# Convolution and SoLU block on one core: the prologue's order recast, w_out's low words on GpSimd, g in the mean's matrix, narrow products for the first eight tiles, the third tile in its own banks

## Chip, core and metric

The kernel runs on one core of a Trainium2 chip, in one launch. The engines named below are TensorE (PE, with its weight loads PEld), VectorE (DVE), ScalarE (ACT), GpSimd (POOL) and the queue of SyncE (SP), which issues the DMAs. The metric is the device time of one execution in microseconds; three executions were timed before the change.

## What is computed

Inputs are x (8 x 4160 x 192, float32), weight (8 heads x 7 taps), w_in (192 x 1024), w_out (1024 x 192) and g_ln (1024); the last three are float64, read by the kernel as pairs of 32-bit words.

```python
# 1. causal convolution over 7 rows, softmax weights per head (24 columns each)
w = softmax(weight, axis=-1)
out = einsum('hk,bskhg->bshg', w, x_unf)
# 2. h = x @ w_in, SoLU, layer norm, second product
h = x @ w_in
solu = h * softmax(h)
ln = (solu - mean(solu)) / sqrt(var(solu) + 1e-6) * g_ln
return (ln @ w_out).astype(float32)
```

## The kernel before

The 33,280 rows are 260 tiles of 128 rows. Each tile passes through these steps, every one a helper with a name: the first product `ph` (PE; `emit_rows` L736 and `emit_third` L759, eight and two or more matmuls of 512 columns), the maximum (`emit_max` L788, DVE), the exponential (`emit_exp` L795, ACT), the numerators h*e (`emit_mul` L805, DVE), their upper half in float16 (`emit_hi` L813, ACT), the lower half (`emit_lo` L825, POOL), a DMA transpose of both, the second product `po` (`emit_out` L841, PE), its evacuation (`emit_evac` L848, DVE), and a scaling per row and a store. All instructions are written out by hand in one order per engine (the schedule is manual), and each engine works through its own list strictly in order; semaphores carry the dependences, those of a buffer that is overwritten too.

The convolution works on chunks of up to 19 windows of 112 rows. Its product `pc` is made on PE (L281), its upper half is stored by ACT (`upper`, L313) and its lower half by DVE (`lower`, L322), and DMA transposes (`turn`, L352) bring both into `yT`, from which the tiles take their rows.

PSUM holds three pairs of banks (`pair(0)` to `pair(2)`), used in turn by the first products and by the convolution's early groups (`hold`), and two single banks for `po` and small sums.

Before the first tile stands a prologue. It makes the tap matrix; it turns the float64 words of w_in into float32 (`wi`: `exponents`, `mantissas`, `join`, `signs`, `value` on DVE; `powers`, `squares` on ACT), finds a power-of-two scale `t_in` from the sum of squares, and writes w_in in two float16 parts, `whi` and `wlo`. The same is done for w_out (`wo`), in part between the first tiles: `exponents` L447 and `mantissas` L452 on DVE, `lows` L458, `powers` L486 and `floats` L463 on ACT, `signs` L489 on DVE, `whole` L474 and `value` L496 on POOL. `signs` writes its result in place over the exponents `e_out`. Then `out_powers` (L685, ACT, eight instructions) multiplies `e_out` by g_ln, `squares` (L469, ACT) sums its squares for the scale `t_out`, a product with the constant matrix `even` gives the mean over rows of w_out (L701, PE), `out_upper` subtracts it (L710, DVE) and writes the upper half `ohi` (L715, ACT), `out_lower` (L719, DVE) the lower half `olo`.

The first eight tiles go two at a time (`first_two`, `second_two`, `third_two`, `fourth_two`), all later ones three at a time (`three_steps`). In `first_two` the tiles 0 and 1 use pairs 0 and 1, and pair 2 takes two groups of chunk 1's convolution; in `second_two` the tiles 2 and 3 use pairs 0 and 1 again. A `po` of a tile in a group of several tiles is 16 matmuls, eight of 384 columns (upper and lower half of w_out side by side) and eight of 192; the five last tiles have groups of one and use 24 matmuls of 192.

Of the kernel before, what the change touches and what calls it, by code (L numbers as in the profile page):

```python
# [19 lines left out]
def kernel(  # L20
# [102 lines left out]
    class Chunk:  # L123
# [185 lines left out]
        def upper(self, pc, h, n, a, b):  # L309

            col, cuts = h * HD, self.cut(h * HD, n * HD)
            for e, z in zip(cuts, cuts[1:]):
                act.activation(  # L313
                    self.at(0, col + e, col + z, a, b), pc[:, :, e:z], AF.Copy,
                    scale=self.scale(),
                )

# [77 lines left out]
    )  # L395

# [22 lines left out]
    even = cp.tile([P, P], F32, name="even")  # L419
    pool.memset(even, 1.0 / F)  # L420
# [6 lines left out]
    class Words:  # L427
# [29 lines left out]
        def lows(self, c, scale):  # L457
            act.activation(  # L458
                self.low[:, c].bitcast(F32), self.low[:, c], AF.Copy, scale=scale
# [5 lines left out]
        def squares(self, c, to):  # L465
# [4 lines left out]
                junk, self.e[:, c].bitcast(F32), AF.Square, scale=2.0**20, accum_out=to  # L470
# [65 lines left out]
    wi.powers(halves[0])  # L536

# [28 lines left out]
    words(halves[1])  # L566
    for h in c0.halves(1):
        c0.sum_squares(*h)
        if h[2] == 0:
            wi.powers(halves[1])  # L570
# [15 lines left out]
    isq = cp.tile([P, 2], F32, name="isq")  # L586
# [8 lines left out]
    def settle(a, z, got):  # L595
        for pc, hg in got:
            c0.lower(pc, *hg)
        for blk in (0, 2, 1):
# [8 lines left out]
    wi.signs(halves[0], wi.m)  # L607
    wi.exponents(Z)
    wi.powers(Z)
    for f in chain0[1:-3]:  # L610
        f()
    wi.squares(Z, isq[:, 1:2])
    for pc, hg in got0:
        c0.upper(pc, *hg)
    wi.value(halves[0], wi.m, dve)
    valued(halves[1])
    c0.open(0, None)
# [50 lines left out]
    def settle_rest():  # L668
        settle(*spans0[1], got0)
# [26 lines left out]
    def out_mean():  # L696
# [827 lines left out]
```

## Time and profile before

| | |
|---|---|
| median of three runs | 1181.34 us (1178.92 to 1181.7) |
| the profiled execution | 1182.51 us, of which the span from first to last instruction is 1180.7 us |
| busy over the span | PE 96%, DVE 87%, ACT 84%, POOL 74% |
| granted TensorE clock | 0.999 of full on average |

The busy shares are averages over two different kernels in one: the long stage of three tiles at a time, and the first 120 us, in which the prologue's work and the first tiles share the engines. The views of the second kind are the windows (busy time of each engine by stretch) and the timelines of single engines.

### The profile page before, as it was taken

How to read it: one execution, taken by the hardware profiler on the slowest of the kernel's cores; microseconds unless marked ns; L12 is line 12 of the kernel's file. 1: busy time of each engine (PE TensorE's matmuls, PEld its weight loads, DVE VectorE, ACT ScalarE, POOL GpSimd, SP SyncE). 2: the span in 40 equal slices, each digit the busy share in tenths (PEclk: the TensorE clock that was granted, in tenths of full speed). 3: DMA queues.
4: the chain of work that ended last, by engine and by line, in shares of the span. 5: the costliest groups of instructions: out<-in, count | busy, mean ns of one | idle time of the engine just before them, and what ended most of it. 6: DMA issues, size and time to landing. Idle time of an engine off the chain costs nothing.

```text
span 1180.7 us, 22219 instructions
## 1 busy us (share of the span) xinstructions
PE 1136.1 (96%) x7678; PEld 688.2 (58%) x7678; DVE 1027.5 (87%) x2072; ACT 997.1 (84%) x1758; POOL 876.7 (74%) x683
## 2 busy tenths in 40 slices
PE   5888999999999999999999999999999999999997
PEld 3455555565566555556556665655566556566555
DVE  7888888898899889898898989888898998788787
ACT  6997888888888888788888888888888888888885
POOL 1644878887978778797867878688788868855664
PEclk9999999999999999999999999999999999999999
DMA  7898899999999999999999999999999998999987
GB/s 196 187 183 157 154 220 200 207 185 204 192 212 205 184 197 186 209 197 197 208 187 214 187 211 200 189 204 192 220 190 194 195 202 167 180 171 193 180 159 174
DMA packets 727294, 226.94 MB, mean 192 GB/s; under 512 B 651518, under 2 KB 725774, under 8 KB 727182
## 3 DMA queue, kind: packets, MB, share of 16 engines
q1 hardware_dynamic: 727182, 225.53, 99.5%
q8 instruction: 60, 0.98, 0.3%
q14 instruction: 52, 0.43, 0.1%
HBM read 33.00 MB, written 25.56 MB: 50 GB/s over the span
## 4 chain that ended last, share of the span: by engine, by line
PE 70%; DVE 7%; DMA 6%; POOL 6%; issue 4%; ACT 4%; SPq 2%; ACTq 0%; POOLq 0%; DVEq 0%
PE po L841 32%; PE ph L736 29%; DMA pT<-p 5%; PE pc L281 4%; PE ph L759 4%; POOL p L825 4%; DVE ph L788 2%; DVE e L805 1%; ACT p L813 1%; DMA raw_in<-in_moe_w_in_dram 1%; SPq L827 1%; POOL t L909 1%; ACT e L795 1%; ACT sq L817 1%; DVE y L322 1%
## 5 line engine op out<-in xcount | busy, mean ns | idle before, releaser
L825 POOL TENSOR_TENSOR p<-e,p 128x1024 f16<-128x1024 f32 x259 | 552.4, 2137 | 243.8 <-ACT p L813 242.7
L841 PE MATMUL po<-ohl,pT 128*128 128x384 f16 (+1 forms) x4200 | 542.3, 285 | 16.3 <-DMA pT<-p 10.8
L841 PEld LDWEIGHTS <-pT 128*128 128x128 f16 x4200 | 380.2, 98 | 181.8 <-DMA pT<-p 13.9
L736 PE MATMUL ph<-whi,yT 128*128 128x512 f16 x1548 | 419.1, 380 | 6.0 <-DVE e L805 4.6
L788 DVE TENSOR_SCALAR_CACHE_REDUCE ph<-ph,cv 128x1024 f32<-128x1024 f32 x248 | 319.2, 1288 | 78.3 <-PE ph L759 61.7
L795 ACT ACTIVATE e<-ph,sm 128x1024 f32<-128x1024 f32 x260 | 289.2, 1112 | 105.2 <-DVE ph L788 98.6
L805 DVE SCALAR_TENSOR_TENSOR e<-ph,cv,e 128x1024 f32<-128x1024 f32 x248 | 317.0, 1278 | 22.6 <-ACT e L795 22.3
L736 PEld LDWEIGHTS <-yT 128*128 128x128 f16 x2064 | 192.4, 98 | 235.0 <-issue 34.9
L813 ACT CAST p<-e 128x1024 f16<-128x1024 f32 x260 | 269.9, 1039 | 39.0 <-DVE e L805 38.8
L817 ACT ACTIVATE sq<-e 128x1024 f32<-128x1024 f32 x260 | 273.5, 1052 | 0.1
L848 DVE TENSOR_REDUCE raw<-po 128x192 f32<-128x384 f32 x255 | 140.6, 552 | 15.9 <-PE po L841 15.6
L736 PE MATMUL ph<-wlo,yT 128*128 128x512 f16 x516 | 153.5, 379 | 0.0
L243 POOL TENSOR_TENSOR xs<-xr,xs 128x960 f16<-128x960 f32 (+1 forms) x56 | 107.5, 1920 | 1.4
L313 ACT ACTIVATE y<-pc 112x432 f16<-112x432 f32 (+5 forms) x140 | 62.7, 469 | 17.4 <-PE pc L281 11.7
L759 PE MATMUL ph<-wlo,yT 64*128 64x512 f16 x269 | 74.1, 380 | 1.1 <-DMA yT<-y 1.1
L281 PE MATMUL pc<-xs,taps_hi 128*112 128x240 f16 (+1 forms) x448 | 72.9, 261 | 1.4 <-DVE xm L203 1.4
L322 DVE SCALAR_TENSOR_TENSOR y<-pc,y 112x432 f16<-112x432 f32 (+5 forms) x140 | 72.2, 532 | 0.7 <-ACT y L313 0.7
L759 PE MATMUL ph<-wlo,y 64*128 64x512 f16 x251 | 68.5, 380 | 1.3 <-DMA y<-yT 1.3
L181 DVE TENSOR_REDUCE xa<-xr 128x1 f32<-128x384 f32 x112 | 66.6, 617 | 3.2 <-DMA xr<-in_x_dram 3.2
L281 PEld LDWEIGHTS <-taps_hi 128*112 128x112 f16 x448 | 52.4, 130 | 18.1 <-issue 1.7
L240 POOL TENSOR_SCALAR xr<-xr,s 128x960 f32<-128x960 f32 (+1 forms) x56 | 57.5, 1026 | 3.0
L281 PE MATMUL pc<-xs,taps_lo 128*112 128x240 f16 (+1 forms) x224 | 58.5, 261 | 0.0
(145 smaller groups left out, 783.9 us busy)
## 6 DMA issues: line engine op xcount, KB each, us to landing
out_dram<-raw SPq DMA_DIRECT2D x127, 192.0 KB, 3.0
xr<-in_x_dram SPq DMA_DIRECT2D x41, 480.0 KB, 5.1
xr<-in_x_dram SPq DMA_DIRECT2D x22, 384.0 KB, 4.1
pT<-p SPq DMA_TRANSPOSE x260, 4.7
y<-yT SPq DMA_DIRECT2D x15, 140.0 KB, 3.0
y<-yT SPq DMA_DIRECT2D x15, 126.0 KB, 3.0
yT<-y SPq DMA_TRANSPOSE x102, 3.7
raw_out<-in_moe_w_out_dram SPq DMA_DIRECT2D x1, 1536.0 KB
```

Of the source, the lines that this page charges most:

```text
L243: (2.1 * size + 0.2, lambda: pool.tensor_tensor(xl, r, h, ALU.subtract)),
L281: nc.tensor.matmul(o, tp[:, h + j, :], r, start=q == 0, stop=q == len(ops) - 1)
L736: nc.tensor.matmul(bank, lhs, w[:, r, n * 512 : (n + 1) * 512], start=start and j == 0, stop=stop and j == len(ops) - 1,)
L759: nc.tensor.matmul(banks_of(t)[n], y[q, t.off : t.off + P], wlo[q, 1, n * 512 : (n + 1) * 512], start=start, stop=not start,)
L788: dve.tensor_scalar(t.ph, t.ph, t.cv[:, 0:1], None, ALU.mult, ALU.min, accum_out=t.bias)
L795: act.activation(t.e, t.ph, AF.Exp, bias=t.bias, scale=-1.0, accum_out=grp.z[:, g : g + 1])
L805: dve.scalar_tensor_tensor(t.e, t.ph, t.cv[:, 3:4], t.e, ALU.mult, ALU.mult, accum_out=t.grp.s1[:, t.g : t.g + 1],)
L813: act.copy(t.p16[:, :, 0, :], t.halves)
L817: act.activation(junk, t.e, AF.Square, accum_out=t.grp.s2[:, t.g : t.g + 1])
L825: eng.tensor_tensor(t.p16[:, :, 1, :], t.halves, t.p16[:, :, 0, :], ALU.subtract)
L841: nc.tensor.matmul(t.po[:, 0:n], t.pT[:, a, :], w, start=j == 0, stop=j == len(ops) - 1)
L848: dve.tensor_reduce(t.grp.raw[:, t.g, :], t.po[:, 0 : 2 * D].rearrange("p (a d) -> p d a", a=2), AX.X, ALU.add,)
```

## The change

- `gl` (g_ln) is loaded right behind w_out instead of after chunk 1. `even` is no longer a constant: it is made on POOL from `gl` (a matrix per block of 128 rows, g/1024), in one of the four `p16` buffers.
- `wo.lows` moves from ACT to POOL, behind the small constants of tile 0.
- In the prologue w_in's first half is finished earlier (`valued(halves[0])`), its squares are taken in three parts, the convolution's first two groups stand together on PE ahead of the sum `pt_x`, the second part's groups ahead of the sum `pt_wi`, and the transposes of block 0 are issued as soon as the upper halves they need are written.
- `out_powers` is gone. `out_squares` takes its place: the largest |g| (two small DVE instructions) is the scale of `wo.squares`, which now stands ahead of `signs` and is written before it. `out_upper` becomes eight instructions of 192 columns with g as scalar instead of two of 768.
- `hold` of chunk 1's first two groups moves from `first_two` to `second_two`, into pair 1; tile 2 uses pair 2, tile 3 pair 0, and the later tiles keep that rotation.
- In `first_two` tile 0's `emit_hi` stands right behind its `emit_mul`, ahead of tile 1's exponential.
- The first eight tiles' `po` is 24 matmuls of 192 columns, and their evacuation a copy instead of a sum of two halves.

```diff
@@ prologue
-    even = cp.tile([P, P], F32, name="even")
-    pool.memset(even, 1.0 / F)
+    even = sp.tile([P, NH, 2, 512], F16, name="even", tag="p16", bufs=4)
...
+    pool.tensor_scalar(
+        even, gl.unsqueeze(2).broadcast_to([P, NFC, P]), 1.0 / F, 1.0,
+        ALU.mult, ALU.mult,
+    )
...
     words(halves[0])
     wi.powers(halves[0])
+    valued(halves[0])
...
-    going = convolve(*spans0[0], [pq[:, 0:512], pq[:, 512:F]])
-    got0 = [next(going)]
+    got0 = list(convolve(*spans0[0], [pq[:, 0:512], pq[:, 512:F]]))
     c0.add_up()
-    got0 += going
-    wi.squares(A, isq[:, 0:1])
...
+    wi.squares(halves[1], isq[:, 1:2])
+    c0.open(0, None)
+    ups = [f for pc, hg in got0 for f in c0.upper_steps(pc, *hg)]
+    for f in ups[:2]:
+        f()
+    c0.turn(0, *spans0[0])
     wi.exponents(Z)
     wi.powers(Z)
+    valued(halves[1])
+    wi.mantissas(Z)
+    wi.squares(Z, isq[:, 2:3])
...
-    wo.lows(W, 2.0**-32)
-    wi.mantissas(Z)
     wi.join(Z)
...
+    wo.lows(W, 2.0**-32)
     wo.mantissas(W)
@@ out_powers, out_upper
-    def out_powers():
-        woe = wo.e.bitcast(F32).rearrange("p (c d) -> p c d", d=D)
-        for j in range(NFC):
-            act.activation(
-                woe[:, j], woe[:, j], AF.Copy, scale=gl[:, j : j + 1]
-            )
+    def out_squares():
+        g = cp.tile([P, 1], F32, name="g_max")
+        dve.tensor_reduce(g, gl, AX.X, ALU.max, apply_absolute_value=True)
+        dve.tensor_scalar(g, g, 2.0**20, None, ALU.mult)
+        wo.squares(W, osq, g)
...
-            dve.scalar_tensor_tensor(
-                wof[:, c], wof[:, c], 1.0,
-                mean[:, 0:D].unsqueeze(1).broadcast_to([P, NFC // 2, D]),
-                ALU.mult, ALU.subtract,
-            )
+            for j in range(c.start, c.stop):
+                dve.scalar_tensor_tensor(
+                    wof[:, j], wof[:, j], gl[:, j : j + 1], mean[:, 0:D],
+                    ALU.mult, ALU.subtract,
+                )
@@ emit_out, emit_evac
+        t.wide = t.grp.n > 1 and t.i >= PAIRED
...
+        if not t.wide:
+            dve.tensor_copy(t.grp.raw[:, t.g, :], t.po[:, 0:D])
@@ first_two
         emit_first(t, u)
-        hold(c, 0)
-        hold(c, 1)
         emit_max(t)
         emit_exp(t)
+        out_squares()
         wo.signs(W, wo.e)
...
-        emit_mul(t)
-        out_powers()
+        numerators(t)
         emit_max(u)
         emit_exp(u)
-        wo.squares(W, osq)
-        emit_hi(t)
         settle_rest()
@@ second_two
         emit_two(t, u)
+        hold(c, 0)
+        hold(c, 1)
```

**Where the instructions stand now.** On DVE, between the exponents of w_out and the numerators of tile 1 (`e_out` the exponents, `ph_0` and `ph_1` the first products of tiles 0 and 1, `e_0` and `e_1` their exponentials), this stood before:

```order
L452 TENSOR_SCALAR m_out_254<-raw_out_74 128x1536
L788 TENSOR_SCALAR ph_0_273,sm_0_304<-ph_0_273,cv_0_166 128x1024
L489 SCALAR_TENSOR_TENSOR e_out_253<-raw_out_74,e_out_253 128x1536
L805 SCALAR_TENSOR_TENSOR e_0_306,s1_0_269<-ph_0_273,cv_0_166,e_0_306 128x1024
L788 TENSOR_SCALAR ph_1_274,sm_1_320<-ph_1_274,cv_0_166 128x1024
```

and this stands there now:

```order
L465 TENSOR_SCALAR m_out_255<-raw_out_74 128x1536
L804 TENSOR_SCALAR ph_0_275,sm_0_297<-ph_0_275,cv_0_169 128x1024
L701 TENSOR_REDUCE g_max_301<-gl_75 128x1
L702 TENSOR_SCALAR g_max_301<-g_max_301 128x1
L503 SCALAR_TENSOR_TENSOR e_out_254<-raw_out_74,e_out_254 128x1536
L821 SCALAR_TENSOR_TENSOR e_0_299,s1_0_271<-ph_0_275,cv_0_169,e_0_299 128x1024
L804 TENSOR_SCALAR ph_1_276,sm_1_312<-ph_1_276,cv_0_169 128x1024
```

Two small instructions are new, and `signs` (the SCALAR_TENSOR_TENSOR on e_out) keeps its place ahead of tile 0's numerators. On ACT, in the same stretch (`oj_out` is the unused result of `squares`, `osq` its sum), this stood before:

```order
L463 CAST m_out_254<-m_out_254 128x1536
L795 ACTIVATE e_0_306,z_0_268<-ph_0_273,sm_0_304 128x1024
L685 ACTIVATE e_out_253<-e_out_253,gl_75 128x192 x8
L795 ACTIVATE e_1_322,z_0_268<-ph_1_274,sm_1_320 128x1024
L469 ACTIVATE oj_out_0_324,osq_267<-e_out_253 128x1536
L813 CAST p16_0_326<-e_0_306 128x2x512
L813 CAST p16_1_336<-e_1_322 128x2x512
```

and this stands there now:

```order
L477 CAST m_out_255<-m_out_255 128x1536
L811 ACTIVATE e_0_299,z_0_270<-ph_0_275,sm_0_297 128x1024
L483 ACTIVATE oj_out_0_304,osq_269<-e_out_254,g_max_301 128x1536
L829 CAST p16_0_310<-e_0_299 128x2x512
L811 ACTIVATE e_1_314,z_0_270<-ph_1_276,sm_1_312 128x1024
L829 CAST p16_1_324<-e_1_314 128x2x512
```

The eight multiplications by g are gone, and `squares` now stands right behind tile 0's exponential. On PE, around the end of tile 3's first product (`pc_1_0` the convolution's held groups, `pt_wo` the sum over partitions for w_out's scale, `ph_4` tile 4's first product), this stood before:

```order
L759 MATMUL ph_3_362<-wlo_105,yT_0_197 128x512
L95 MATMUL pt_wo_373<-osq_267,ones_99 128x1
L701 MATMUL mean_379<-f_out_198,even_101 128x192 x8
L736 LDWEIGHTS yT_0_197
L736 MATMUL ph_4_432<-whi_104,yT_0_197 128x512
```

and this stands there now:

```order
L775 MATMUL ph_3_350<-wlo_106,yT_0_190 128x512
L281 MATMUL pc_1_0_361<-xr_1_0_228,taps_135 112x5x24 x8
L95 MATMUL pt_wo_370<-osq_269,ones_100 128x1
L717 MATMUL mean_376<-f_out_203,even_102 128x192 x8
L752 LDWEIGHTS yT_0_190
L752 MATMUL ph_4_435<-whi_105,yT_0_190 128x512
```

The held groups have come in between tile 3's product and the sum; before, they stood ahead of tile 2's product.

## Rows read from the trace of the kernel before

**Rows 1.** Windows: busy us of PE, PEld, DVE, ACT, POOL; clock; DMA share; GB/s.

```profile
30.00:60.00 30.00, 25.12 (x140) 13.06 (x139) 26.65 (x52) 28.55 (x53) 21.00 (x12) 1.00 0.88 186
90.00:120.00 30.00, 26.18 (x170) 16.02 (x170) 25.28 (x55) 22.93 (x43) 15.63 (x17) 0.94 0.83 164
180.00:1150.00 970.00, 960.82 (x6515) 579.10 (x6513) 854.97 (x1699) 829.57 (x1453) 759.40 (x579) 1.00 1.03 194
```

**Rows 2.** Chain of waits, 24 to 62 us: start, us, engine and what.

```profile
31.79 2.87 ACT e_out L685 x8
...
37.13 1.90 PE ph L736 x8
```

**Rows 3.** Timeline of PE, 0 to 48 us: start, length, line, operation.

```profile
10.63 1.94 PE L281 MATMUL pq<-xr,taps 128*112 128x120 f32 x8 [1.07 <-ACT taps L561]
15.53 0.56 PE L95 MATMUL pt_x<-xa,ones 128*128 128x4 f32 x2 [2.96 <-ACT xj L187]
...
28.96 1.89 PE L281 MATMUL pc<-xr,taps 128*112 128x120 f32 x16
...
39.74 2.85 PE L701 MATMUL mean<-f_out,even 128*128 128x192 f32 x16
```

**Rows 4.** Timeline of DVE, 0 to 48 us.

```profile
13.88 0.42 DVE L452 TENSOR_SCALAR m_in<-raw_in 128x512 int32<-128x512 int32 x1
14.33 0.69 DVE L480 SCALAR_TENSOR_TENSOR f_in<-raw_in,m_in 128x512 f32<-128x512 uint32 x1
...
28.55 1.29 DVE L788 TENSOR_SCALAR_CACHE_REDUCE ph<-ph,cv 128x1024 f32<-128x1024 f32 x1
...
29.75 1.76 DVE L489 SCALAR_TENSOR_TENSOR e_out<-raw_out,e_out 128x1536 int32<-128x1536 int32 x1
31.63 1.28 DVE L805 SCALAR_TENSOR_TENSOR e<-ph,cv,e 128x1024 f32<-128x1024 f32 x1
...
35.78 1.28 DVE L805 SCALAR_TENSOR_TENSOR e<-ph,cv,e 128x1024 f32<-128x1024 f32 x1 [0.27 <-ACT e L795]
...
42.70 1.82 DVE L710 SCALAR_TENSOR_TENSOR f_out<-f_out,mean 128x768 f32<-128x768 f32 x2
44.44 1.28 DVE L805 SCALAR_TENSOR_TENSOR e<-ph,cv,e 128x1024 f32<-128x1024 f32 x1
```

**Rows 5.** Timeline of ACT, 0 to 48 us.

```profile
21.09 1.63 ACT L458 ACTIVATE raw_out<-raw_out 128x1536 f32<-128x1536 uint32 x1
...
30.34 1.10 ACT L795 ACTIVATE e<-ph,sm 128x1024 f32<-128x1024 f32 x1
...
35.65 1.47 ACT L469 ACTIVATE oj_out<-e_out 128x1536 f16<-128x1536 f32 x1
```

**Rows 6.** Timeline of POOL, 0 to 48 us.

```profile
27.67 1.44 POOL L208 TENSOR_SCALAR cv<-cv 128x1 f32<-128x1 f32 x3 [22.81 <-DVE cv L205]
...
31.85 3.54 POOL L474 TENSOR_TENSOR f_out<-m_out,raw_out 128x1536 f32<-128x1536 f32 x1
35.47 3.45 POOL L496 TENSOR_TENSOR f_out<-f_out,e_out 128x1536 f32<-128x1536 f32 x1
```

**Rows 7.** Groups by line and shape: busy us, mean ns, idle before.

```profile
L848 DVE TENSOR_REDUCE raw<-po 128x192 f32<-128x384 f32 x255 | 140.6, 552 | 15.9 <-PE po L841 15.6
L322 DVE SCALAR_TENSOR_TENSOR y<-pc,s,y 112x160 f16<-112x160 f32 x5 | 1.9, 383 | 3.0 <-ACT y L313 3.0
L871 DVE TENSOR_SCALAR e<-po,t,o_inv 128x192 f32<-128x192 f32 x3 | 1.4, 477 | 3.3 <-PE po L841 2.7 <-POOL t L863 0.7
```

**Rows 8.** Timeline of PE at the end: the two forms of po.

```profile
1153.60 2.12 PE L841 MATMUL po<-ohl,pT 128*128 128x384 f16 x16
...
1168.18 2.15 PE L841 MATMUL po<-ohl,pT 128*128 128x192 f16 x24 [0.27 <-DMA pT<-p]
```

**Rows 9.** Windows of 2 us around one wait of PE, columns as in Rows 1.

```profile
112.00:114.00 2.00, 0.29 (x2) 0.11 (x2) 1.92 (x9) 2.00 (x5) 1.38 (x2) 0.91 0.46 95
114.00:116.00 2.00, 2.00 (x10) 1.26 (x9) 2.00 (x5) 2.00 (x8) 1.55 (x6) 0.50 1.13 228
```

More of the change, by code (lines that the diff above doesn't have):

```diff
@@ L307, in cut, with upper_steps @@
             return [0, P - col, width] if col < P < col + width else [0, width]
-        def upper(self, pc, h, n, a, b):
+        def upper_steps(self, pc, h, n, a, b):
             col, cuts = h * HD, self.cut(h * HD, n * HD)
-            for e, z in zip(cuts, cuts[1:]):
-                act.activation(
+            return [
+                lambda e=e, z=z: act.activation(
                     self.at(0, col + e, col + z, a, b), pc[:, :, e:z], AF.Copy,
@@ L316, in upper @@
                 )
+                for e, z in zip(cuts, cuts[1:])
+            ]
+        def upper(self, *group):
+            for f in self.upper_steps(*group):
+                f()
         def lower(self, pc, h, n, a, b):
@@ L457, in lows @@
         def lows(self, c, scale):
-            act.activation(
-                self.low[:, c].bitcast(F32), self.low[:, c], AF.Copy, scale=scale
+            pool.tensor_scalar(
+                self.low[:, c].bitcast(F32), self.low[:, c], scale, 1.0,
+                ALU.mult, ALU.mult,
             )
@@ L463, in floats, with squares @@
             act.copy(self.m[:, c].bitcast(F32), self.m[:, c])
-        def squares(self, c, to):
+        def squares(self, c, to, scale=2.0**20):
             junk = sp.tile([P, F], F32, name=f"oj_{self.name}_{c.start}", tag="sq", bufs=1)
@@ L469, in squares @@
             act.activation(
-                junk, self.e[:, c].bitcast(F32), AF.Square, scale=2.0**20, accum_out=to
+                junk, self.e[:, c].bitcast(F32), AF.Square, scale=scale, accum_out=to
             )
@@ L565 @@
         )
-    words(halves[1])
+    isq = cp.tile([P, 3], F32, name="isq")
+    wi.squares(halves[0], isq[:, 0:1])
     for h in c0.halves(1):
         c0.sum_squares(*h)
-        if h[2] == 0:
-            wi.powers(halves[1])
+    wi.exponents(halves[1])
+    wi.powers(halves[1])
     def split_taps(q):
@@ L597, in settle @@
             c0.lower(pc, *hg)
-        for blk in (0, 2, 1):
+        for blk in (2, 1):
             c0.turn(blk, a, z)
     pq = pair(1, "pq")
-    going = convolve(*spans0[0], [pq[:, 0:512], pq[:, 512:F]])
-    got0 = [next(going)]
+    got0 = list(convolve(*spans0[0], [pq[:, 0:512], pq[:, 512:F]]))
     c0.add_up()
-    got0 += going
-    wi.squares(A, isq[:, 0:1])
-    wi.signs(halves[0], wi.m)
+    for f in chain0[1:-3]:
+        f()
+    wi.mantissas(halves[1])
+    wi.join(halves[1])
+    wi.squares(halves[1], isq[:, 1:2])
+    c0.open(0, None)
+    ups = [f for pc, hg in got0 for f in c0.upper_steps(pc, *hg)]
+    for f in ups[:2]:
+        f()
+    c0.turn(0, *spans0[0])
     wi.exponents(Z)
     wi.powers(Z)
-    for f in chain0[1:-3]:
-        f()
[L612 to L617, printed above, removed]
+    valued(halves[1])
+    wi.mantissas(Z)
+    wi.squares(Z, isq[:, 2:3])
+    for f in ups[2:]:
+        f()
     got1 = got0
     wo, W = Words(raw_out, "out"), slice(0, NFC * D)
-    tp = total(isq, "wi")
     got0 = list(convolve(*spans0[1], [single("pr_0"), single("pr_1")]))
+    tp = total(isq, "wi", pair(2, "pt_wi")[:, 0:512])
     dve.tensor_reduce(isq[:, 0:1], tp, AX.X, ALU.add)
@@ L701, in out_mean @@
             nc.tensor.matmul(
-                mean[:, 0:D], even, wof[:, c, :],
+                mean[:, 0:D], even[:, c], wof[:, c, :],
                 start=(c == 0), stop=(c == NFC - 1),
@@ L764, in emit_two @@
     def emit_two(t, u):
-        for slot, q in enumerate((t, u)):
+        for slot, q in ((2, t), (0, u)):
             q.ph = pair(slot, f"ph_{q.i}")
@@ L1123, in hold @@
         if j % 2 == 0:
-            c.held = pair(2, f"pc_{c.ch}_{j}")
+            c.held = pair(1, f"pc_{c.ch}_{j}")
         bank = c.held[:, j % 2 * 512 : (j % 2 + 1) * 512]
```

23 lines of the change are left out of this document (12 added, 11 removed).

## Prediction

> **What bounds the kernel now.** I read the windows first, to see which stage the change can reach. From 180 to 1150 us, with three tiles at a time, PE is busy 960.82 of 970 us; DVE, ACT and POOL have room there [rows 1]. The change touches nothing in that stage but the names of its banks, and its columns per tile stay what they were. So the whole difference must come from the first 120 us. There no engine is the bound by itself: from 30 to 60 us ACT is busy 28.55 of 30 us, DVE 26.65 and PE 25.12; from 90 to 120 us PE 26.18, DVE 25.28, ACT 22.93 [rows 1]. Such a stretch is a chain from engine to engine, and what an edit is worth is read from the link that ends last. After the start-up the work of each engine is in a fixed order, so a delay of all engines at 45 us arrives as a delay of the end unless a later link gets shorter.
>
> The chain of waits names the links: around 32 us it goes through the eight multiplications by g on ACT (2.87 us), later through tile 3's product on PE (1.90 us and its rest), which had to wait until tile 1's banks were free [rows 2]. These are the links that the change removes. The timelines of the single engines then tell what else is near. On DVE tile 0's maximum starts at 28.55, `signs` at 29.75 (1.76 us), tile 0's numerators at 31.63, tile 1's at 35.78, `out_upper` at 42.70, tile 3's numerators at 44.44 [rows 4]. On ACT tile 0's exponential starts at 30.34, w_out's squares at 35.65 [rows 5]. POOL joins w_out from 31.85, in 3.54 and 3.45 us [rows 6], and PE makes the mean from 39.74 in 2.85 us [rows 3].
>
> **The start, to tile 0's maximum.** PE now makes both convolution groups in a row: 10.63 plus twice 1.94 is 14.5, so `pt_x` starts there instead of at 15.53 [rows 3], and the scale that waits for it is 1.0 us earlier. But in DVE's list three instructions of 512 columns now stand between that scale and the last squares of w_in (mantissas and join of the second half, exponents of the rest: 0.42, 0.69 and again about 0.42 [rows 4]), 1.5 us, and `t_in` waits for those squares. That is 0.5 us later for `t_in`. Behind it DVE has one mantissas less (0.42). I take 0 for tile 0's maximum; the bounds are a gain of 1.0 (the whole of `pt_x`) and a loss of 0.5. That w_out's low words leave ACT (1.63 us [rows 5]) brings nothing here: the next ACT work, the rest of w_in's upper part, waits for the DVE work just told. On POOL they follow the constants of tile 0, which end at 29.11 [rows 6]; the unseen duration there lies between 0 and that of the two-operand pass of the same size, 3.54 [rows 6], so they end by 32.7, before POOL's next work can start (below, 35.2). `gl` and the larger `even` are hidden by POOL's idle time of 22.81 us before 27.67 [rows 6]; without that cover the loss would be the pass over 1024 elements, at most 3.54.
>
> **The wait that comes in.** `squares` of w_out now reads `e_out` before `signs` overwrites it in place. So `signs` on DVE can't start until ACT has done it, and in ACT's list it stands behind tile 0's exponential: 30.34 plus 1.10 plus 1.47, with the two readings of the accumulators about 33.1 [rows 5]. Before, `signs` ran beside the exponential, from 29.75 [rows 4]. Now it runs from 33.1 to 34.9, 3.4 us late. DVE stands still from about 30.2. Queued behind it on DVE are tile 0's numerators, tile 1's maximum and the rest of the convolution; POOL waits for the signs to join w_out. Tile 0's numerators start at 34.9 instead of 31.63, +3.3. Tile 1's exponential no longer waits for the multiplications by g, but it stands behind tile 0's upper half, which needs the numerators: 34.9 plus 1.28, about 1.0 for the upper half, 1.3 for the exponential, so tile 1's numerators start near 38.7 instead of 35.78, +2.9, and end at 40.0.
>
> **Whether the new banks win it back.** Tile 2's product no longer waits (pair 2 is free) and tile 3's waits for tile 0's numerators only, so both maxima can follow tile 1's numerators at once. But behind the products, on PE, stand the held groups (pair 1, free at 40.0), 1.89 us [rows 3], then the sum for `t_out` and the mean. And the mean waits for POOL: 35.2 plus 3.54 plus 3.45 [rows 6] is 42.3. Both paths meet at 42.3, and the mean ends at 45.2 instead of 42.6. The early products are thus hidden work. `out_upper` starts at 45.3 instead of 42.70, +2.6.
>
> **out_upper in eight pieces.** Before, two of 768 columns took 1.82 us [rows 4]. The bounds for eight of 192 are 1.82 (cost by columns only) and 3.8 (eight times the 0.477 of a 192-column pass from PSUM [rows 7]). The nearest row is the 160-column pass of the same operation with a scalar per partition, 0.383 [rows 7]; less some 0.03 that neighbours overlap, eight take 2.8. I take that: +1.0. The Trainium skill speaks against such splitting: VectorE: DVE Perf Modes, the section on the trn2 errata, says that the fixed latency is paid per instruction, so many small tiles pay it each time. Its PSUM formula gives an estimate of 0.325 us for 192 columns, 2.6 for eight, and a sum 0.2 lower than mine; the rows above agree with the direction. With mine, tile 3's numerators start at 48.1 instead of 44.44: +3.6.
>
> **The narrow products.** At the end of the program both forms of `po` stand: 24 of 192 take 2.15 us, 16 pieces 2.12 [rows 8]. That is 8 x 0.03 = 0.2 us on PE, in a stretch where PE waits for others: 0. The evacuations shrink from a reduction of 384 columns, 0.552 [rows 7], to a copy of 192. Its price is between half of that (0.276) and the 0.477 of the 192-column pass [rows 7]; near the 160-column pass, 0.35, it saves 0.2 a tile, 1.6 for eight. DVE is busy 26.65 and 25.28 of 30 us in these stretches [rows 1], so not every one lies on the chain; I count half, -0.8, with bounds of -0.3 and -2.2.
>
> **The sum.** 0 + 3.6 - 0.8 = +2.8 us. The profiled execution took 1182.51 us, 1.8 more than its span of 1180.7, and would take 1185.3. The runs' median is 1181.34, 1.2 below the profiled one; so I forecast 1184.1 for the median. The bounds of the terms reach from -0.6 (start -1.0, `out_upper` no dearer, evacuations all on the chain) to +4.8.
>
> **The rivals.** *The mean runs at half clock* (slower). PE now has a gap: tile 2's product is done near 31, tile 3's can't start before 36.2. One row shows what a gap can do: PE was busy 0.29 of 2 us at 112 to 114, and the clock stood at 0.50, 1.2 GHz, for the next 2 [rows 9]. The mean's 2.85 us, on the chain, would become up to 5.7: +2.85, so 1187.0. It decides if the clock is still low at 42.3. Against it: PE works from 36.2 on, and the gaps before 33 and 37 us in the trace of before left the clock at 1.00 [rows 1]. The Trainium skill's TensorE: Matmul & The Clock Gate, in its table on why this matters, warns of idle gaps between bursts of matmuls; by that rule the fall itself is likely, and whether it lasts to the mean no row tells. Chance 0.12.
>
> *The links taken out are simply gone* (faster). ACT is the busiest engine from 30 to 60 us [rows 1], and 2.87 and 1.90 us leave the chain [rows 2]. If the squares' wait costs nothing, the time falls by 4.8 and by the evacuations' 0.8, to 1175.7. Against it stands the fixed order: `signs` reads and overwrites what the squares read. Chance 0.10.
>
> *The delay wears off before the long stage.* PE has 3.8 us of idle time from 90 to 120 us [rows 1]. If these waits are for something that does not move with the tiles, the lost 3.6 is absorbed there, and the saved 0.8 remains at best: 1180.5. Against it: DVE and ACT, for which PE waits, are behind by the same amount. Chance 0.15.
>
> **How the numbers follow.** My forecast has 0.55, the three rivals 0.12, 0.10 and 0.15, and 0.08 is left for what I don't see. 0.3%, about what a measurement of this kernel can tell from no change, is 3.5 us. Of the forecast's 0.55 I put 0.17 beyond +3.5; with the first rival and a part of the rest, slower has 0.31; faster has the second rival and a little, 0.12; within 0.3% remain 0.57. The range is 1179.0 to 1188.0: down to the worn-off case and the spread of the runs, up to the half clock. The forecast's own range is 1181 to 1186.5.
>
> **What the profile after would show.** On DVE an idle time of about 3 us before `signs`, put down to ACT's squares; tile 0's numerators near 35; on PE tile 2's product right behind tile 1's and a gap of some 5 us; the mean from 42 to 45; copies of about 0.35 us in place of the first eight evacuations; the long stage as before. I am wrong if `signs` starts near 30, if the mean starts before 40, or if tile 3's numerators stand late and the long stage nevertheless begins no later.

## The result and the profile after

| | before | after |
|---|---|---|
| median of 19 runs each | 1180.43 us | 1182.15 us (1180.52 to 1186.18) |
| ratio | | 1.0021, 95% interval 1.0011 to 1.0031 |
| profiled execution, and its span | 1182.51, 1180.7 us | 1181.38, 1179.7 us |
| granted TensorE clock, mean | 0.999 | 0.994 |

The changed kernel is slower by 0.21%, 1.3 to 3.7 us by the interval; the forecast for its median was 1184.1 us. Its profiled execution is nevertheless 1.1 us *shorter* than that of before, which lay 2 us above its kernel's median. So the two traces are compared by stretch, not by their ends.

The windows of after, columns as in [rows 1]:

```profile
30.00:60.00 30.00, 24.20 (x137) 13.63 (x136) 24.68 (x54) 23.07 (x40) 18.65 (x11) 0.89 0.74 155
90.00:120.00 30.00, 25.85 (x187) 16.92 (x188) 26.60 (x58) 23.62 (x45) 13.28 (x14) 1.00 0.89 158
180.00:1150.00 970.00, 963.27 (x6532) 580.72 (x6530) 857.57 (x1701) 831.08 (x1457) 762.03 (x580) 1.00 1.02 195
```

From 30 to 60 us ACT is busy 5.5 us less and DVE 2.0 less than in [rows 1], and PE 0.9. ACT lost 2.87 us of work there; that DVE and PE are less busy too means that they wait. The timeline of DVE shows for what, answering to [rows 4]:

```profile
17.31 0.42 DVE L465 TENSOR_SCALAR m_in<-raw_in 128x512 int32<-128x512 int32 x1
...
27.49 1.29 DVE L804 TENSOR_SCALAR_CACHE_REDUCE ph<-ph,cv 128x1024 f32<-128x1024 f32 x1 [0.17 <-PE ph L775]
...
31.80 1.76 DVE L503 SCALAR_TENSOR_TENSOR e_out<-raw_out,e_out 128x1536 int32<-128x1536 int32 x1 [2.75 <-ACT oj_out L483]
33.48 1.28 DVE L821 SCALAR_TENSOR_TENSOR e<-ph,cv,e 128x1024 f32<-128x1024 f32 x1
...
37.30 1.28 DVE L821 SCALAR_TENSOR_TENSOR e<-ph,cv,e 128x1024 f32<-128x1024 f32 x1
...
44.69 2.69 DVE L727 SCALAR_TENSOR_TENSOR f_out<-f_out,gl,mean 128x192 f32<-128x192 f32 x8 [0.85 <-PE mean L717]
47.30 1.28 DVE L821 SCALAR_TENSOR_TENSOR e<-ph,cv,e 128x1024 f32<-128x1024 f32 x1
```

Tile 0's maximum (27.49) is 1.06 us early, then `signs` waits 2.75 us for ACT's `squares`, tile 1's numerators are 1.52 late, `out_upper` 1.99 and tile 3's numerators 2.86. The timeline of ACT confirms the order that makes the wait, answering to [rows 5]: `squares` follows the exponential at once.

```profile
29.02 1.10 ACT L811 ACTIVATE e<-ph,sm 128x1024 f32<-128x1024 f32 x1
...
30.12 1.56 ACT L483 ACTIVATE oj_out<-e_out,g_max 128x1536 f16<-128x1536 f32 x1
```

The timeline of PE, answering to [rows 3]:

```profile
10.33 3.25 PE L281 MATMUL pq<-xr,taps 128*112 128x120 f32 x16 [1.07 <-ACT taps L576]
13.42 0.29 PE L95 MATMUL pt_x<-xa,ones 128*128 128x4 f32 x2
...
34.82 1.04 PE L752 MATMUL ph<-whi,yT 128*128 128x512 f16 x2 [3.94 <-DVE e L821]
...
39.31 2.44 PE L281 MATMUL pc<-xr,taps 128*112 128x120 f32 x16
41.59 0.29 PE L95 MATMUL pt_wo<-osq,ones 128*128 128x1 f32 x2
41.74 2.85 PE L717 MATMUL mean<-f_out,even 128*128 128x192 f32 x16
```

PE stands still 3.94 us ahead of tile 3's product. What the clock does around that is in five windows. The value behind the five busy times is the granted clock; a stretch in which it falls to 0.50 is called a dip below.

```profile
14.00:19.00 5.00, 1.83 (x17) 1.65 (x16) 4.37 (x16) 2.81 (x7) 1.03 (x1) 1.00 0.63 159
20.00:26.00 6.00, 5.14 (x13) 1.58 (x12) 5.87 (x9) 4.45 (x8) 0.00 (x0) 0.50 0.57 136
27.00:33.00 6.00, 3.89 (x16) 1.04 (x14) 3.04 (x6) 4.77 (x6) 2.29 (x4) 1.00 1.10 329
34.00:40.00 6.00, 5.18 (x13) 1.86 (x14) 6.00 (x13) 3.30 (x4) 5.92 (x2) 0.50 0.23 44
41.00:47.00 6.00, 5.84 (x36) 4.15 (x34) 4.31 (x16) 4.73 (x10) 6.00 (x3) 1.00 0.95 209
```

Twice PE had little to do (1.83 of 5 us from 14 to 19; nothing from 30.9 to 34.8), and in the next stretch the clock is at 0.50, 1.2 GHz. In the kernel before PE is busy 3.35 of 5 us from 14 to 19, and from 20 to 26 its clock is at 1.00. The second dip lengthens the held groups from 1.89 [rows 3] to 2.44 us; POOL's last pass for the mean ends at 40.97 (below), so the mean starts 0.77 us later than it could. The mean itself runs at full clock again. POOL's timeline, answering to [rows 6]:

```profile
17.97 1.06 POOL L430 TENSOR_SCALAR even<-gl 128x1024 f32<-128x1024 f32 x1 [13.24 <-DMA gl<-in_moe_g_ln_dram]
...
27.74 1.63 POOL L471 TENSOR_SCALAR raw_out<-raw_out 128x1536 f32<-128x1536 uint32 x1
...
37.53 3.44 POOL L510 TENSOR_TENSOR f_out<-f_out,e_out 128x1536 f32<-128x1536 f32 x1
```

`even` and the low words (17.97, 27.74) find POOL idle, as predicted; what they do to DVE the experiments tell. The groups by shape show the new evacuation, 0.347 us against the 0.552 of [rows 7]:

```profile
L866 DVE COPY raw<-po 128x192 f32<-128x192 f32 x8 | 2.7, 347 | 0.0
```

Where the lag goes later is read from the starts of the tiles' exponentials on ACT (us; last column tile 4 less tile 0). They stand here for all kernels of this study, one profiled execution each:

| kernel | tile 0 | tile 1 | tile 4 | tile 8 | tile 16 | 4 less 0 |
|---|---|---|---|---|---|---|
| before | 30.34 | 34.56 | 50.15 | 69.89 | 112.93 | 19.81 |
| after | 29.02 | 36.06 | 52.94 | 72.34 | 115.40 | 23.92 |
| after_again | 29.84 | 36.89 | 53.06 | 73.59 | 116.90 | 23.22 |
| signs_first | 29.41 | 34.15 | 50.04 | 69.45 | 112.73 | 20.63 |
| fill_gap | 29.59 | 36.64 | 52.82 | 72.23 | 115.28 | 23.23 |
| wide_all | 29.85 | 36.90 | 53.80 | 73.56 | 116.61 | 23.95 |
| new_start_only | 29.71 | 34.73 | 50.31 | 70.06 | 113.12 | 20.60 |
| lows_early | 29.85 | 33.85 | 49.74 | 70.27 | 113.52 | 19.89 |
| old_banks | 29.86 | 36.90 | 53.34 | 72.74 | 115.77 | 23.48 |
| two_passes | 29.31 | 36.36 | 52.53 | 71.93 | 115.20 | 23.22 |
| quiet_pool | 29.66 | 33.78 | 49.91 | 69.31 | 112.57 | 20.25 |
| halves_and_mean | 29.62 | 33.74 | 50.28 | 69.71 | 112.77 | 20.66 |
| one_pass_waits | 29.41 | 33.30 | 48.36 | 67.76 | 110.82 | 18.95 |
| both_wait | 29.43 | 33.32 | 49.30 | 68.70 | 112.39 | 19.87 |

After less before is -1.32 at tile 0, +2.79 at tile 4, +2.45 at tile 8 and +2.47 at tile 16. 2.47 us is 0.21% of the time, which is also the measured ratio. Between tiles 16 and 23 the profiled execution of before then loses 2.7 us against that of after (39.73 us against 37.06), so that tile 23 starts level, at 152.66 and 152.46. In before the `po` at 113.7 ran at half clock [rows 9]; in after the like wait left the clock at 1.00. That is a matter of the execution: in after_again, a second profile of the same kernel, that `po` falls into a dip, as its windows show:

```profile
116.00:118.00 2.00, 0.32 (x3) 0.25 (x3) 1.91 (x9) 2.00 (x5) 1.40 (x1) 0.98 0.89 205
118.00:120.00 2.00, 2.00 (x11) 1.30 (x9) 2.00 (x5) 2.00 (x8) 1.55 (x6) 0.50 1.13 230
```

The other profiles agree. The stretch from tile 16 to tile 23 takes 37.06 to 38.11 us in the four without a dip between 112 and 122 us (after, signs_first, wide_all, one_pass_waits) and 38.54 to 40.35 us in the ten with one. So this difference between the two traces is no gain of the change.

### The profile page after: what moved, and what is told of

The parts are those of the page before. It is cut to its first block, busy times and chain, and to the rows that moved or that the text cites. A ratio compares the mean times of both kernels' runs of the same rounds, so it can differ in the third digit from the quotient of the medians.

```text
span 1179.7 us, 22346 instructions
## 1 busy us (share of the span) xinstructions
PE 1137.1 (96%) x7742; PEld 691.0 (59%) x7742; DVE 1027.4 (87%) x2080; ACT 993.9 (84%) x1751; POOL 879.7 (75%) x684
## 4 chain that ended last, share of the span: by engine, by line
PE 74%; DVE 7%; POOL 5%; DMA 5%; issue 4%; ACT 4%; SPq 1%; ACTq 0%; POOLq 0%; DVEq 0%
PE po L858 33%; PE ph L752 31%; PE pc L281 5%; PE ph L775 5%; DMA pT<-p 4%; POOL p L841 3%; DVE ph L804 2%; ACT p L829 1%; DVE e L821 1%; ACT e L811 1%; POOL t L929 1%; ACT sq L833 1%; POOL xr L240 1%; DVE y L328 1%; POOL xs L243 1%
## 5 line engine op out<-in xcount | busy, mean ns | idle before, releaser
L858 PE MATMUL po<-ohl,pT 128*128 128x192 f16 (+1 forms) x4264 | 540.9, 283 | 16.7 <-DMA pT<-p 10.6
L868 DVE TENSOR_REDUCE raw<-po 128x192 f32<-128x384 f32 x247 | 136.2, 551 | 14.4 <-PE po L858 14.1
```

Of the source, the lines that this page charges most:

```text
L858: nc.tensor.matmul(t.po[:, 0:n], t.pT[:, a, :], w, start=j == 0, stop=j == len(ops) - 1)
L868: dve.tensor_reduce(t.grp.raw[:, t.g, :], t.po[:, 0 : 2 * D].rearrange("p (a d) -> p d a", a=2), AX.X, ALU.add,)
```

## The experiments

The theory is that of the prediction: `signs` waits for `squares`, and that delay arrives at the end. The rivals are the clock, the dearer `out_upper`, and a delay that wears off. Ratios are to the kernel before, measured beside each on the same chip; they are estimated from the single runs and are not the quotients of the two medians.

| kernel | median, runs | before | ratio, interval |
|---|---|---|---|
| signs_first | 1180.93, 12 | 1180.79 | 1.0013, 1.0000 to 1.0026 |
| fill_gap | 1186.55, 6 | 1180.79 | 1.0046, 1.0030 to 1.0062 |
| wide_all | 1183.51, 12 | 1180.79 | 1.0025, 1.0015 to 1.0034 |
| new_start_only | 1183.13, 12 | 1180.79 | 1.0019, 1.0007 to 1.0031 |
| lows_early | 1180.10, 12 | 1181.28 | 0.9992, 0.9979 to 1.0004 |
| old_banks | 1183.84, 11 | 1181.28 | 1.0026, 1.0017 to 1.0035 |
| two_passes | 1183.84, 12 | 1181.28 | 1.0023, 1.0012 to 1.0034 |
| after_again | 1184.16, 12 | 1181.28 | 1.0012, 1.0000 to 1.0025 |
| quiet_pool | 1181.39, 12 | 1180.45 | 0.9997, 0.9983 to 1.0010 |
| halves_and_mean | 1181.36, 12 | 1180.45 | 0.9999, 0.9983 to 1.0014 |
| one_pass_waits | 1180.14, 12 | 1179.86 | 1.0001, 0.9989 to 1.0013 |
| both_wait | 1179.38, 12 | 1179.86 | 0.9993, 0.9980 to 1.0006 |

**signs_first.** The wait turned round.

```diff
-        out_squares()
         wo.signs(W, wo.e)
+        out_squares()
```

> The changed kernel with signs ahead of the squares in the code, so that the squares on ACT wait for the signs on DVE and no longer the other way round. If the 2.75 us that DVE stands still before signs is what the change loses, signs starts at about 28.9, right behind tile 0's maximum, tile 0's numerators at 30.9 instead of 33.48, tile 1's at 34.9 instead of 37.30, tile 3's at 44.0 to 44.9 instead of 47.30, and the median falls by 2.4 to 3.3 us, from 1182.15 to about 1179.3, at or just below the kernel before. If such a delay wears off before the long stage (the rival of the prediction), or if something behind it (the mean, out_upper) holds tile 3's numerators at 47, the median stays within 0.5 us of 1182.15, and tile 16's exponential starts where it did.

Tile 4's exponential starts 3.29 us sooner after tile 0's than in after (20.63 against 23.92), at the upper end of what was expected; against after_again, the second profile of the same kernel, it is 2.6. But DVE's timeline holds a surprise:

```profile
28.87 2.47 DVE L503 SCALAR_TENSOR_TENSOR e_out<-raw_out,e_out 128x1536 int32<-128x1536 int32 x1
```

`signs` stands right behind the maximum now, and takes 2.47 us where it took 1.76. On POOL's timeline, beside it:

```profile
28.14 1.62 POOL L471 TENSOR_SCALAR raw_out<-raw_out 128x1536 f32<-128x1536 uint32 x1
```

The median came to 1180.93 where 1179.3 was expected, and the ratio's interval still overlaps that of after. By the ratio alone this run would not decide.

**lows_early.** signs_first with the low words moved on POOL.

```diff
     wo, W = Words(raw_out, "out"), slice(0, NFC * D)
+    wo.lows(W, 2.0**-32)
...
-    wo.lows(W, 2.0**-32)
     wo.mantissas(W)
```

> The kernel of signs_first with w_out's low words set on GpSimd at once behind the larger matrix of means, some 8 us earlier. In signs_first, signs took 2.47 us instead of 1.76 while GpSimd's pass over the low words ran beside it from 28.14 to 29.76. If the two slow each other, signs takes 1.76 us here, every start behind it comes 0.7 us earlier (out_upper 11.7 us after tile 0's exponential starts instead of 12.4, unless the mean's wait for the held groups keeps 0.3 of it), the copy to float32 on DVE at about 20.3 us becomes longer than its 0.69, and the median lies 0.4 to 0.7 below signs_first's, near 1180.4. If it is not the neighbour but the earlier position of signs itself that made it longer, signs stays at 2.4 to 2.5 us and nothing moves.

DVE's timeline:

```profile
29.30 1.74 DVE L503 SCALAR_TENSOR_TENSOR e_out<-raw_out,e_out 128x1536 int32<-128x1536 int32 x1
```

`signs` is at 1.74 again, `out_upper` starts 11.65 us after tile 0's exponential, as expected, 4 less 0 is 19.89 against 19.81 before, and the ratio, 0.9992, lies with its interval below the first one of after. With these two edits the loss is gone: it came from `signs`' place, and from POOL's pass beside it where that place was mended. The runs on this kernel's chip say the same: the three kernels there that keep the wait (after_again, old_banks, two_passes) have medians of 1183.84 to 1184.16 us, lows_early 1180.10. The expected longer copy at 20 us did not come: DVE was then at its pass over the convolution's PSUM banks.

**fill_gap.** After, with tile 2's product made three times.

```diff
     def emit_two(t, u, again=0):
...
+            for _ in range(again if q is t else 0):
+                emit_rows(q, True, True)
...
-        emit_two(t, u)
+        emit_two(t, u, 2)
```

> The changed kernel with tile 2's product made three times instead of once (it starts over each time, so the value is the same), which fills PE's gap of 3.94 us before tile 3's product with some 3.5 us of work. If the clock fell to half at 33.5 because PE stood still from 30.9 to 34.8, the granted clock is 1.00 from 27 us on, tile 3's product takes 2.7 us instead of 4.6, the held groups 1.89 instead of 2.44, the mean starts with POOL's last joined half at 41.0 instead of 41.74, and the median falls by 0.8 to about 1181.4. The rival, that the gap was not the cause or that the mean waits for POOL anyway: the clock dips as before or the mean's start moves by less than 0.2, and the median stays at 1182.1.

The window of the second dip:

```profile
34.00:40.00 6.00, 3.95 (x21) 1.68 (x20) 6.00 (x12) 3.04 (x4) 5.62 (x3) 1.00 0.28 32
```

The timeline of PE:

```profile
39.27 1.86 PE L281 MATMUL pc<-xr,taps 128*112 128x120 f32 x16 [1.44 <-issue]
...
41.60 2.87 PE L717 MATMUL mean<-f_out,even 128*128 128x192 f32 x16 [0.34 <-POOL f_out L510]
```

The dip is gone and the mean waits for POOL: the pause did cause it, and 4 less 0 is 0.69 lower than in after. But after_again, with its dip from 32 to 40 us, has 23.22 too, since there the clock is up before the held groups start. So the second dip costs some 0.8 us ahead of the mean, as in after, or nothing, by the execution. The median was expected to fall by 0.8 and rose by 4.4 us over after, though from tile 4 on all starts to tile 16 lie within 0.2 us of after's. The profiled run was the shortest of the six (1182.91 to 1186.90), so what the longer ones lost is not shown.

**wide_all.** After, with the wide form for all tiles.

```diff
-        t.wide = t.grp.n > 1 and t.i >= PAIRED
+        t.wide = t.grp.n > 1
```

> The changed kernel with the products of the first eight tiles in the wide form again, with their reduction as evacuation. If the copies save what the prediction counted (half of eight times 0.2 us), the median rises by 0.8, to 1183.0, with bounds of 0.3 and 1.6; the tiles from the ninth on start that much later. The rival, that none of them lies on the chain: 1182.1, and no start moves by more than 0.2 us.

From tile 4 to tile 8 it takes 19.76 us where after takes 19.40: the copies are worth 0.4, not 0.8, and nothing more is added by tile 16 (62.81 against 62.46 from tile 4). The other profiles agree: 19.40 to 19.43 us with copies, 19.74 and 19.75 with reductions (before, new_start_only); only after_again and lows_early, which have a dip near 50 us, take 20.53. The ratio does not tell wide_all from after.

**new_start_only.** Before, with the prologue's edits and `lows` on POOL alone (the diff of the section on the change, without the parts from `even`, out_powers on).

> The kernel before with the recast start alone (both convolution groups in a row, the new order of w_in's words, gl loaded early, w_out's low words on GpSimd); multiplications by g, banks, out_upper and products as before. If the 1.06 us by which tile 0's maximum is early in the changed kernel comes from the start, it stands at 27.5 here too, the whole program follows, and the median falls from 1180.4 to about 1179.4. The rival, that it wears off by 120 us: 1180.4. The clock should dip from about 20 to 27 us as in the changed kernel, if the pause of PE after its early convolution is the cause, and not dip from 33 to 40.

Tile 0 is 0.63 us earlier than before, and at tile 1 that is gone: `signs` meets POOL's low words and takes longer.

```profile
29.13 2.54 DVE L497 SCALAR_TENSOR_TENSOR e_out<-raw_out,e_out 128x1536 int32<-128x1536 int32 x1
```

So the start brings nothing by tile 16 (113.12 against 112.93). The dip at 18 to 26 us came, as expected; one at 32 to 36 came too, which was not. That the kernel measures 0.19% slower than before is not explained by its first 115 us. This run stands against the theory as an account of the whole time: without the wait it measures nearly the ratio of the changed kernel. Its profiled run, 1182.07, is among the shorter ones, and the cause stays open.

**old_banks.** After, with the banks of before.

```diff
-        for slot, q in ((2, t), (0, u)):
+        for slot, q in enumerate((t, u)):
...
-            c.held = pair(1, f"pc_{c.ch}_{j}")
+            c.held = pair(2, f"pc_{c.ch}_{j}")
...
         emit_first(t, u)
+        hold(c, 0)
+        hold(c, 1)
```

> The changed kernel with the banks of before: tile 2's product in pair 0, tile 3's in pair 1, the held convolution groups in pair 2 right behind tile 1's product. If the early products are hidden work, as the prediction said, the mean still waits for GpSimd's joined words (41.0) or at most for tile 3's product (about 41.3), out_upper starts within 0.5 us of 15.7 us after tile 0's exponential, and the median stays within 0.6 us of the changed kernel's. If the new banks are worth the 1.90 us that the chain of waits of before shows for tile 3's product, out_upper and tile 4's exponential start 1.5 to 2 us later and the median rises by as much.

`out_upper` starts at 45.09, 15.23 us after tile 0's exponential (after 15.67, after_again 14.98), and 4 less 0 is 23.48, between the two. Its median, 1183.84, is 0.3 below after_again's on the same chip. The new banks are hidden work, as predicted.

**two_passes.** After, with `out_upper` in two instructions; it leaves out the multiplication by g.

```diff
-            for j in range(c.start, c.stop):
-                dve.scalar_tensor_tensor(
-                    wof[:, j], wof[:, j], gl[:, j : j + 1], mean[:, 0:D], ...
+            dve.scalar_tensor_tensor(
+                wof[:, c], wof[:, c], 1.0,
+                mean[:, 0:D].unsqueeze(1).broadcast_to([P, NFC // 2, D]), ...
```

> The changed kernel with out_upper in two instructions of 768 columns, as before; the multiplication by g is left out, so w_out is scaled by nothing. If the eight pieces cost what the trace says (2.69 against 1.82), tile 4's exponential starts 23.0 us after tile 0's instead of 23.9, and the median falls by 0.9 to about 1181.3. If ACT's two conversions, which follow each half, or the rest of the chain hide it, nothing moves.

```profile
45.15 1.82 DVE L726 SCALAR_TENSOR_TENSOR f_out<-f_out,mean 128x768 f32<-128x768 f32 x2 [0.86 <-PE mean L717]
46.88 1.28 DVE L821 SCALAR_TENSOR_TENSOR e<-ph,cv,e 128x1024 f32<-128x1024 f32 x1
```

Numerators 1.73 us behind `out_upper`'s start instead of 2.61: these 0.88 us are on the chain, and 4 less 0 is 23.22 (23.0 expected, 23.92 in after), with a dip as dear as in after. The median, 1183.84 against after_again's 1184.16, doesn't show it.

**after_again.** The changed kernel once more.

> The changed kernel once more, for comparison on the same chip: 1.0011 to 1.0031 times the kernel before, tile 4's exponential 23.9 us after tile 0's, the clock low from 20 to 27 and from 33 to 41 us, and no wait that the first profile lacks. If the dips belong to one execution and not to the order of the work, one of them is missing or stands elsewhere.

Both dips came, and three more (at 49, 90 and 117 us); tile 0's exponential starts 0.82 us later than in the first profile. A cause of 0.45 stands in DVE's timeline:

```profile
17.69 1.28 DVE L465 TENSOR_SCALAR m_in<-raw_in 128x512 int32<-128x512 int32 x1
```

and in POOL's:

```profile
17.42 1.27 POOL L430 TENSOR_SCALAR even<-gl 128x1024 f32<-128x1024 f32 x1 [12.70 <-DMA gl<-in_moe_g_ln_dram]
```

When gl arrives decides: in after `even` began at 17.97, behind the mantissas, which took 0.42; here it began ahead of them. They take 1.28, and `t_in` comes 0.45 late. Of the eight traces so far with this `even`, five show it (the ninth that the next expectation counts, new_start_only, has no such pass).

**quiet_pool.** signs_first, with gl ahead of w_out, the largest g found early, and the low words behind a copy of one element.

```diff
+    nc.sync.dma_start(gl, g_ln.rearrange("(c p) -> p c", p=P))
     nc.sync.dma_start(
         raw_out.rearrange("p (c d) t -> p c (d t)", d=D),
...
+    pool.tensor_copy(gate_in, isq[0:1, 0:1])
+    wo.lows(W, 2.0**-32)
```

> The kernel of signs_first with GpSimd's two long passes put where DVE doesn't read two operands: gl is loaded ahead of w_out, so that the larger matrix of means is made before 14 us; the low words start behind a copy of one element of w_in's sum, at about 19; and the largest g is found while DVE waits for pt_x. In five of nine executions so far DVE's last mantissas of w_in took 1.28 us instead of 0.42 where GpSimd's pass of 1024 columns ran beside them. If that sharing is the cause, the mantissas take 0.42, t_in's last step starts at 19.2 or earlier, tile 0's exponential at 29.0 to 29.4, signs takes 1.76 and out_upper starts 11.4 to 11.7 us after that exponential; the median is 0.2 to 0.5 below lows_early's, at 0.998 to 0.999 of the kernel before. If it is not, the mantissas still show 1.28 in this trace or the start doesn't come earlier for it, and the median stays at lows_early's 0.9992.

The mantissas take 0.42 and `signs` 1.75: both collisions are gone. Still tile 0's exponential starts at 29.66 and the median is no lower. In DVE's timeline the next wait stands. Tile 0's product lies in the first dip, which in the traces so far had cost DVE 0.28 us at most there:

```profile
28.28 1.29 DVE L806 TENSOR_SCALAR_CACHE_REDUCE ph<-ph,cv 128x1024 f32<-128x1024 f32 x1 [0.54 <-PE ph L777]
```

**halves_and_mean.** quiet_pool, with the join in halves, the held groups behind the mean, and tile 3's product made twice.

```diff
-        wo.whole(W)
+        for h in HW:
+            wo.whole(h)
...
         out_mean()
+        hold(c, 0)
+        hold(c, 1)
```

> quiet_pool with w_out joined in two halves on GpSimd (so that the first half of the mean's products can run beside the second half's pass), with the held groups behind the mean, and with tile 3's product made twice, so that PE has no long pause ahead of the mean. If the mean's wait for GpSimd is the last link ahead of out_upper (DVE stands still 0.76 us there in lows_early), out_upper starts 10.6 to 10.9 us after tile 0's exponential, tile 4's exponential 18.8 to 19.2 us after it, and the median falls by 0.7 to 1.0 against quiet_pool, to about 0.9975 of the kernel before. If something else is last (the held groups now late for the third pair of tiles, or PE's clock in the mean), tile 6's exponential doesn't come earlier than in quiet_pool, and the median is the same.

`out_upper` starts at 40.55, 10.93 us after tile 0's exponential, and yet tile 4 is later. DVE's timeline:

```profile
40.55 2.69 DVE L730 SCALAR_TENSOR_TENSOR f_out<-f_out,gl,mean 128x192 f32<-128x192 f32 x8
43.15 1.28 DVE L826 SCALAR_TENSOR_TENSOR e<-ph,cv,e 128x1024 f32<-128x1024 f32 x1
44.35 4.32 DVE L738 SCALAR_TENSOR_TENSOR ohl<-f_out,t_out,ohl 128x768 f16<-128x768 f32 x2
```

and POOL's:

```profile
38.72 6.33 POOL L846 TENSOR_TENSOR p<-e,p 128x1024 f16<-128x1024 f32 x3
45.65 2.21 POOL L846 TENSOR_TENSOR p<-e,p 128x1024 f16<-128x1024 f32 x1 [0.60 <-ACT p L834]
```

`out_upper` and the numerators, with one operand in PSUM, run beside POOL's passes at their usual length; `out_lower`, with two in SBUF, takes 4.32 us instead of the 1.95 of quiet_pool and gives back what was won. The ratio, 0.9999, misses the 0.9975 that was expected.

**one_pass_waits and both_wait.** halves_and_mean, with POOL's low half of tile 3 (the first), or of tiles 2 and 3 (the second), behind `out_lower`.

```diff
-        for q in (t, u):
-            emit_lo(q, pool)
+        emit_lo(t, pool)
+        pool.tensor_copy(gate, olo[0:1, NFC - 1, 0:1])
+        emit_lo(u, pool)
```

> halves_and_mean with GpSimd's low half of tile 3 behind a copy of one element of out_lower's result. In halves_and_mean out_upper came 1.1 us earlier, but out_lower took 4.32 us instead of 1.95: GpSimd's passes over the tiles ran beside it nearly all the time (to 45.05 and from 45.65 to 47.86). If DVE's pass over two operands waits for GpSimd, out_lower takes 0.7 us (to 45.05) and its 1.95, some 2.6 to 2.7, tile 4's exponential starts 19.0 us after tile 0's instead of 20.66, and the median is 1 to 1.7 us below halves_and_mean's, at 0.9985 to 0.999 of the kernel before. If something else makes out_lower long (its earlier place, the copies on ACT), it stays above 4 us.

> halves_and_mean with GpSimd's low halves of tiles 2 and 3 both behind a copy of one element of out_lower's result. By the same theory out_lower takes 1.95 us, tile 4's exponential starts 18.3 us after tile 0's, 2.3 us earlier than in halves_and_mean, and the median is 1.5 to 2.3 us lower, at 0.998 of the kernel before. If the low halves, 2 and 4 us late now, hold up the products of tiles 2 and 3, tile 6's and tile 8's exponential don't come earlier than in one_pass_waits, and the median is the same as there or higher.

DVE's timeline of one_pass_waits:

```profile
43.92 2.29 DVE L738 SCALAR_TENSOR_TENSOR ohl<-f_out,t_out,ohl 128x768 f16<-128x768 f32 x2
```

DVE's timeline of both_wait:

```profile
44.87 1.94 DVE L738 SCALAR_TENSOR_TENSOR ohl<-f_out,t_out,ohl 128x768 f16<-128x768 f32 x2
```

4.32, 2.29, 1.94: the length follows how much of POOL's work runs beside it. one_pass_waits reaches tile 4 in 18.95 us, the shortest of all. In both_wait that execution had a dip at 32 to 36 us, which made tile 3's maximum wait 0.74 us; `out_upper`, queued behind it on DVE, starts 11.63 us after tile 0's exponential instead of one_pass_waits' 10.71, and 4 less 0 (19.87) misses the 18.3. Neither beats the kernel before by more than the interval (1.0001; 0.9993), though 0.9985 to 0.999 and 0.998 were expected. Against the changed kernel, the intervals of lows_early, quiet_pool and both_wait lie below its first one, but overlap that of after_again.

## Why the prediction came out as it did

- **The wait that comes in: right.** Counted from tile 0's exponential, `signs` was forecast at +2.76 us and came at +2.78, tile 0's numerators at +4.56 and came at +4.46, tile 1's at +8.36 and came at +8.28. signs_first shows that it reaches tile 4, and lows_early that without it the loss to the kernel before is gone.
- **The new banks: right**, by old_banks. The meeting point at 42.3 was off: the mean started at 41.74, with the whole program 1.3 us early and 0.77 us lost to the dip.
- **out_upper in eight pieces: right**, 2.69 us for a forecast of 2.8, and on the chain (two_passes). The estimate of 2.6 us by the Trainium skill's VectorE: DVE Perf Modes, trn2 errata, is 0.09 below the trace; the direction of its rule held.
- **The narrow products: right in kind, half in size.** They bring 0.4 us instead of 0.8 (wide_all); a copy of 0.347 us was forecast as 0.35.
- **The start: the term that was mis-sized.** Forecast 0, measured -1.06 at tile 0's maximum in the first profile, -0.49 in after_again (28.06). Both sides of my sum were off: PE made both groups in 3.25 us instead of twice 1.94, so that `pt_x` came 2.1 us earlier and not 1.0; and "hidden by POOL's idle time" asked only whether POOL was free, not whether DVE and POOL could run side by side. `even` did cost, 0.45 us in five of eight executions, and the low words would have cost 0.7 us (signs_first) had `signs` not been waiting already.
- **The sum.** From -1.06 at tile 0's maximum to +1.85 at its numerators (the wait), +1.52 at tile 1's (the multiplications by g no longer hold up its exponential), +1.99 at `out_upper`, +2.86 behind its eight pieces, less 0.4 by the evacuations: +2.47 at tile 16, where +2.8 was forecast. The ratio gives 1.3 to 3.7. That the sum is off by only 0.3 is in part luck: the early start (-1.3 at tile 0's exponential), the dip (+0.8), the pieces (-0.1) and the smaller gain of the evacuations (+0.4) nearly cancel. The forecast of 1184.1 lies some 2 us above the measured 1182.15: 0.9 of that is the kernel before (1181.34 in three runs, 1180.43 in nineteen), the rest the difference (2.8 forecast, 1.7 between the medians).
- **Half clock, the slower rival: half right.** The pause brought the dip (fill_gap), but it ended before the mean and took 0.8 us by the held groups in after, none in after_again. The Trainium skill's TensorE: Matmul & The Clock Gate warned of such gaps; here the fall agrees, and its price was about a quarter of the rival's 2.85 us.
- **Links simply gone: wrong.** The squares' wait cost 2.75 us on DVE, and ACT, without the multiplications, was busy 23.07 of 30 us instead of 28.55.
- **The delay wears off: not up to tile 16** (+2.79, +2.45, +2.47). Behind that it stays open in part. From the 41st to the 251st exponential the same instructions took between 900.2 us (lows_early) and 903.0 us (two_passes) in the 14 profiles. The clock is at 1.00 there in all of them; what differs is PE's wait for the DMA transposes that `po` reads. From 227 to 1128 us, total, times and longest wait in lows_early, then in two_passes:

```profile
PE po L858 <- DMA pT<-p: 3.8, 6, 1.5
PE po L858 <- DMA pT<-p: 6.9, 9, 1.2
```

So gains and losses of 2 us at 115 us were not found again one to one in the medians (one_pass_waits: 2.1 us ahead of before at tile 16, ratio 1.0001; new_start_only: level, 1.0019). Whether the edits move these waits, or each execution does, is not shown.

## What to carry to other kernels

When work is moved to an idle engine, ask with whom it shares, not only whether the engine is free: list what DVE does with operands in SBUF while POOL's pass runs. When an edit lets one instruction read what another overwrites in place, the order between them is a new wait; put the one that others queue behind first. And a difference of 2 us that one trace shows at a tenth of the program needs the ratio of many runs before it counts: here later waits of PE alone differ by 3 us from trace to trace.

## What the runs showed of the hardware

In these traces DVE and POOL hold each other up where DVE reads its operands from SBUF. `signs` took 1.76 us alone and 2.47 or 2.54 with a POOL pass begun 0.7 us ahead of it; mantissas of one operand 0.42 and 1.28; `out_lower` 1.94 and 4.32. The one that begins second waits, and its wait stands in the trace as a longer instruction: in quiet_pool POOL's low half of tile 3, begun at 46.76 inside `out_lower` (45.47, 1.95 us), took 2.64 us, not 2.13.

```profile
46.76 2.64 POOL L843 TENSOR_TENSOR p<-e,p 128x1024 f16<-128x1024 f32 x1 [1.86 <-ACT p L831]
```

DVE instructions with an operand in PSUM kept their length beside POOL (numerators, 1.27 to 1.29 us in every trace). The Trainium skill's SBUF — State Buffer, section on who interferes with whom, says that the pair of ports that the two engines share is locked for a whole instruction, and whichever is issued second is blocked. These traces agree, and the prediction had not drawn on it.

Between 18 and 28 us the clock fell to 1.2 GHz in every trace of a kernel with the recast start and stayed at 1.00 in the trace of before. Later dips came in some executions and not in others of the same kernel: after_again has one at 118 us, after none.
